# A group norm kernel on one core: one weight load for all the identity matmuls instead of one before each

## The chip, the cores and the metric

The kernel runs on one core of one Trainium2 chip, with the other cores idle. The metric is the device time of one execution in microseconds.

## The reference, cut to what matters

```python
x: (128, 1024, 32, 16) bf16;  g, b: (1024,) bf16;  G = 32 groups
xr  = x.reshape(B, G, C // G, H, W)
mu  = xr.mean(axis=(2, 3, 4));  var = ((xr - mu) ** 2).mean(axis=(2, 3, 4))
out = (xr - mu) / sqrt(var + 1e-5) * g + b          # bf16
```

The input is 134 MB and the output as much again. Each byte must be read once and written once.

## The kernel before

The work is cut into 32 tiles of 128 partitions by 16384 elements (4 MiB). Each partition is one (image, group) pair. Six slots of a ring hold the tiles; each is loaded, normalised in place and stored. For the mean, each partition's row has to be summed. TensorE does part of that: it multiplies by the identity matrix and accumulates twelve chunks of 512 columns in PSUM (the memory that TensorE writes its sums to), so that 6144 columns become 512. VectorE folds the other 10240 columns into one number beside them ("pair sum"), and ScalarE adds up the 513 results. Then ScalarE makes the sum of squares in two halves and VectorE scales the tile in place.

```python
NT = 32; SLOTS = 6; PE_CHUNKS = 12; MM_FREE = 512; PS_BUFS = 3

# SyncE: load(j) -> ring slot j % 6; store(i) waits for done, then writes; six stores are queued at the end

def on_tensor(e):
    e.wait_ge(s_eye, 2)
    e.wait_ge(s_gb, 32)
    e.matmul(out=gb_p[:], lhsT=rep[:], rhs=gb_b[:], start=True, stop=True).then_inc(s_gbp, 1)

    def one(c, t):                                   # tile of slot c in round t
        for k in range(PE_CHUNKS):
            if k == 0:
                e.wait_ge(ld[c], (t + 1) * 16)       # the tile has landed
            elif k == PE_CHUNKS - 2:
                e.wait_ge(meaned[(c - 2) % SLOTS], t + 1)
            elif k == PE_CHUNKS - 1:
                e.wait_ge(paired, t * SLOTS + (c + 1))   # VectorE's pair sum is there
            mm = e.matmul(
                out=sums(c), lhsT=eye[:],
                rhs=slot(c)[:, k * MM_FREE : (k + 1) * MM_FREE],
                start=(k == 0), stop=(k == PE_CHUNKS - 1),
            )                                        # emits a weight load and a matmul
            if k == 0:
                mm.then_inc(first_in, 1)             # lets VectorE start the pair sum
        mm.then_inc(summed[c], 1)                    # lets ScalarE take the mean
    in_rounds(e, one)

# ScalarE per tile: wait summed; mean; square of half 0; square of half 1; variance; square root
# VectorE per tile i: pair(i + 1); wait for the root of tile i; scale and bias; 32 x tensor_scalar in place
# ... (cut)
```

## Time and profile before

| | before |
|---|---|
| device time, median of the first 3 runs | 632.58 us (632.29 to 632.61) |
| profiled span | 631.1 us |
| DMA, share of the span | 99.0%, 268.44 MB |
| VectorE / ScalarE / TensorE busy | 84% / 80% / 25% |
| weight loads | 385, 49.9 us busy |

The page of the kernel before starts with busy times (PE is the matmuls, PEld the weight loads that run beside them, DVE is VectorE, ACT ScalarE, POOL GpSimd), then the span in 40 slices, then the DMA queues, then the groups of instructions. A group line has busy time and mean duration in ns, and behind the second bar the idle time before it and what ended it ("issue" where the profile shows nothing that was waited for). `ring` holds the tiles, `eye` is the identity, `ps` the sums, `jp` belongs to the pair sum and `jm` to the mean:

```profile
span 631.1 us, 2973 instructions
PE 158.2 (25%) x380; PEld 49.9 (8%) x385; DVE 529.4 (84%) x1185; ACT 504.0 (80%) x258; POOL 1.0 (0%) x8
...
DMA  8999999999999999999999999999999999999996
GB/s 366 432 432 413 434 434 430 438 432 432 432 432 432 430 432 432 434 430 434 432 432 428 432 432 430 432 432 432 426 432 432 432 434 432 434 434 434 438 410 263
...
q1 hardware_dynamic: 9648, 268.44, 99.0%
...
L184 PE MATMUL ps<-ring,eye 128*128 128x512 bf16 x379 | 158.0, 589 | 423.9 <-DVE jp L243 292.0
...
L184 PEld LDWEIGHTS ps<-ring,eye 128*128 128x128 bf16 x384 | 49.8, 137 | 531.8 <-DVE jp L243 313.5
```

Read it so: DMA is full in every slice but the first and the last, at 410 to 438 GB/s in all of these. TensorE idles 424 us before its matmuls, and the larger part of that ends when VectorE's pair sum arrives. (Five matmul records are missing from this trace: 379 of 384.)

A burst in the timeline of the kernel before: the twelfth matmul of one tile, which waited for the pair sum, and behind it the first eleven of the next (start, duration, engine, line, what, count; in brackets the idle time in front). The granted clock in this stretch was 0.50:

```profile
53.45 0.13 PEld L184 LDWEIGHTS ps<-ring,eye 128*128 128x128 bf16 x2 [17.26 <-DVE jp L243]
53.46 5.30 PE L184 MATMUL ps<-ring,eye 128*128 128x512 bf16 x12 [16.77 <-DVE jp L243]
...
53.86 0.15 PEld L184 LDWEIGHTS ps<-ring,eye 128*128 128x128 bf16 x1 [0.28 <-issue]
...
54.29 0.15 PEld L184 LDWEIGHTS ps<-ring,eye 128*128 128x128 bf16 x1 [0.27 <-issue]
```

The loads follow each other every 0.43 us, are 0.15 us long, and leave 0.28 us in between. Twelve matmuls in 5.30 us are eleven steps of 0.427 us and one whole duration of 0.61 us. The question is whether the 0.427 us contain any of the load.

The chain of waits of the kernel before, in the tail (start, duration, what):

```profile
522.30 29.25 DMA ring<-in_x_dram
551.55 0.04 issue
551.60 0.62 PE ps L184
...
592.66 0.62 PE ps L184
593.30 0.70 ACT jm L205 x2
```

Here the last tiles are computed with no more loads to come. The chain meets TensorE at a tile's first matmul and at twelfth matmuls that follow a wait, each 0.62 us long.

### The profile page before, as it was taken

How to read it: one execution, taken by the hardware profiler on the slowest of the kernel's cores; microseconds unless marked ns; L12 is line 12 of the kernel's file. 1: busy time of each engine (PE TensorE's matmuls, PEld its weight loads, DVE VectorE, ACT ScalarE, POOL GpSimd, SP SyncE). 2: the span in 40 equal slices, each digit the busy share in tenths (PEclk: the TensorE clock that was granted, in tenths of full speed). 3: DMA queues.
4: the chain of work that ended last, by engine and by line, in shares of the span. 5: the costliest groups of instructions: out<-in, count | busy, mean ns of one | idle time of the engine just before them, and what ended most of it. 6: DMA issues, size and time to landing. Idle time of an engine off the chain costs nothing.

```text
span 631.1 us, 2973 instructions
## 1 busy us (share of the span) xinstructions
PE 158.2 (25%) x380; PEld 49.9 (8%) x385; DVE 529.4 (84%) x1185; ACT 504.0 (80%) x258; POOL 1.0 (0%) x8
## 2 busy tenths in 40 slices
PE   1523333222233330331063014203220430052000
PEld 0101111000010110110011001101000110010000
DVE  1579999999999999699689959995998699599963
ACT  0798999999999999699948977894999499859960
POOL 0000000000000000000000000000000000000000
PEclk9766555666665665666565557656665665576555
DMA  8999999999999999999999999999999999999996
GB/s 366 432 432 413 434 434 430 438 432 432 432 432 432 430 432 432 434 430 434 432 432 428 432 432 430 432 432 432 426 432 432 432 434 432 434 434 434 438 410 263
DMA packets 9744, 268.44 MB, mean 425 GB/s; under 512 B 1168, under 2 KB 1168, under 8 KB 1168
## 3 DMA queue, kind: packets, MB, share of 16 engines
q1 hardware_dynamic: 9648, 268.44, 99.0%
q10 hardware_dynamic: 96, 0.00, 0.0%
HBM read 134.22 MB, written 134.22 MB: 425 GB/s over the span
## 4 chain that ended last, share of the span: by engine, by line
ACT 50%; DMA 34%; DVE 6%; issue 5%; PE 2%; DVEq 2%; SPq 0%
ACT ja L213 46%; DMA out_dram<-ring 18%; DMA ring<-in_x_dram 16%; DVE ring L276 5%; PE ps L184 2%; ACT jm L205 2%; DVEq L259 1%; ACT var L223 1%; ACT std L227 1%; DVE jp L243 1%; DVEq L262 0%; DVEq L264 0%; DVE bia L270 0%; DVE scl L266 0%; DVEq L243 0%
## 5 line engine op out<-in xcount | busy, mean ns | idle before, releaser
L213 ACT ACTIVATE ja<-ring,nm 128x8192 fp8e5<-128x8192 bf16 x64 | 455.8, 7122 | 2.1
L276 DVE TENSOR_SCALAR ring<-ring,scl,bia x1024 | 333.5, 405 | 1.2
L184 PE MATMUL ps<-ring,eye 128*128 128x512 bf16 x379 | 158.0, 589 | 423.9 <-DVE jp L243 292.0
L243 DVE SCALAR_TENSOR_TENSOR jp<-ring 128x5120 fp8e5 (+1 forms) x32 | 175.7, 5492 | 61.4 <-PE ps L184 49.4
L205 ACT ACTIVATE jm<-ps 128x513 fp8e5<-128x513 f32 x32 | 19.3, 602 | 99.0 <-PE ps L184 99.0
L184 PEld LDWEIGHTS ps<-ring,eye 128*128 128x128 bf16 x384 | 49.8, 137 | 531.8 <-DVE jp L243 313.5
L264 DVE RECIPROCAL rstd<-std 128x1 f32 x32 | 6.3, 196 | 11.9 <-ACT std L227 11.9
L213 ACT ACTIVATION_READ_ACCUMULATOR ja<-ring,nm 128x1 f32 x64 | 11.9, 186 | 0.0
L270 DVE SCALAR_TENSOR_TENSOR bia<-scl,nm,gb 128x32 f32<-128x32 f32 x32 | 8.0, 250 | 4.2
L227 ACT ACTIVATE std<-sq,var 128x1 f32<-128x1 f32 x32 | 9.4, 295 | 1.0
L223 ACT ACTIVATE var<-sq,eps_t 128x1 f32<-128x1 f32 x32 | 9.4, 294 | 1.0
L255 DVE COPY gb<-gb_p 128x64 f32<-128x64 f32 x1 | 0.2, 225 | 11.3 <-PE gb_p L173 11.3
L266 DVE TENSOR_SCALAR scl<-gb,rstd 128x32 f32<-128x32 f32 x32 | 7.7, 241 | 1.1
L205 ACT ACTIVATION_READ_ACCUMULATOR jm<-ps 128x1 f32 x32 | 6.2, 194 | 0.0
L243 DVE DVE_READ_ACCUMULATOR jp<-ring (+1 forms) x32 | 4.5, 140 | 0.0
L173 PE MATMUL gb_p<-gb_b,rep 32*128 32x64 bf16 x1 | 0.2, 207 | 11.1 <-DMA gb_b<-in_b_dram 11.1
L201 ACT ACT_TABLE_LOAD x1 | 1.3, 1283 | 1.9 <-issue 1.9
L173 PEld LDWEIGHTS gb_p<-gb_b,rep 32*128 32x128 bf16 x1 | 0.1, 100 | 11.1 <-issue 11.1
L155 POOL TENSOR_SCALAR_AFFINE_SELECT rep<-ones_b 32x128 bf16<-32x128 bf16 x1 | 0.3, 304 | 0.0
L151 POOL TENSOR_SCALAR_AFFINE_SELECT eye<-ones_b 128x128 bf16<-128x128 bf16 x1 | 0.3, 294 | 0.4 <-issue 0.4
L201 ACT ACTIVATE warm<-eps_t 128x1 f32<-128x1 f32 x1 | 0.2, 203 | 0.0
L145 POOL MEMSET ones_b<- 128x128 bf16 x1 | 0.2, 205 | 0.5 <-SPq L283 0.5
(5 smaller groups left out, 0.5 us busy)
## 6 DMA issues: line engine op xcount, KB each, us to landing
ring<-in_x_dram SPq DMA_DIRECT2D x32, 4096.0 KB, 29.2
out_dram<-ring SPq DMA_DIRECT2D x31, 4096.0 KB, 31.5
out_dram<-ring SPq DMA_DIRECT2D x4, 1024.0 KB, 6.9
gb_b<-in_g_dram ACTq DMA_DIRECT2D x1, 2.0 KB, 6.3
gb_b<-in_b_dram ACTq DMA_DIRECT2D x1, 2.0 KB, 9.5
```

Of the source, the lines that this page charges most:

```text
L184: mm = e.matmul(out=sums(c), lhsT=eye[:], rhs=slot(c)[:, k * MM_FREE : (k + 1) * MM_FREE], start=(k == 0), stop=(k == PE_CHUNKS - 1),)
L201: e.activation(out=warm[:], in_=eps_t[:], func=ACT.Sqrt)
L205: e.activation(out=jm[:], in_=sums_and_pairs(c), func=ACT.Identity, scale=-inv_n, accum_out=nm[:, c : c + 1], saturate=False,).then_inc(me ...
L213: e.activation(out=ja[:], in_=slot(c)[:, h * (F // 2) : (h + 1) * (F // 2)], func=ACT.Square, bias=nm[:, c : c + 1], scale=1.0, accum_out= ...
L223: e.activation(out=var[:], in_=sq[:, 0:1], func=ACT.Identity, bias=eps_t[:], scale=inv_n).then_inc(varred[c], 1)
L227: e.activation(out=std[:, c : c + 1], in_=sq[:, 1:2], func=ACT.Sqrt, bias=var[:], scale=inv_n).then_inc(stded, 1)
L243: e.scalar_tensor_tensor(out=jp[:], in0=part(i, lo, n), scalar=1.0, in1=part(i, lo + n, n), op0=ALU.mult, op1=ALU.add, accum_out=ps[:, bas ...
L259: e.drain()
L264: e.reciprocal(out=rstd[:], in_=std[:, bass.ds(i % SLOTS, 1)]).then_inc(inverted, 1)
L266: e.tensor_scalar(out=scl[:], in0=gb[:, 0:KC], scalar1=rstd[:], scalar2=None, op0=ALU.mult).then_inc(scaled, 1)
L270: e.scalar_tensor_tensor(out=bia[:], in0=scl[:], scalar=nm[:, bass.ds(i % SLOTS, 1)], in1=gb[:, KC : 2 * KC], op0=ALU.mult, op1=ALU.add,). ...
L276: ts = e.tensor_scalar(out=a, in0=a, scalar1=scl[:, k : k + 1], scalar2=bia[:, k : k + 1], op0=ALU.mult, op1=ALU.add,)
```

## The change

The identity is always the same weight matrix, so it need not be loaded again for each matmul. The intent is to take 383 of 385 weight loads out of TensorE's stream. The matmuls are emitted as bare instructions that use whatever weights are in the array (with two loads for 385 matmuls the result is correct).

```diff
+        e.ldweights(eye[:])
+
+        def add_up(to, chunk, k):
+            return e.add_instruction(
+                mybir.InstMatmult(
+                    name=nc.get_next_instruction_name(), engine=e.engine,
+                    start_tensor_calc=(k == 0),
+                    stop_tensor_calc=(k == PE_CHUNKS - 1),
+                    ins=[e.lower_ap(chunk), e.lower_ap(eye[:])],
+                    outs=[e.lower_ap(to)],
+                    tile_size=(P, P), tile_position=(0, 0),
+                    ldweights=False,
+                )
+            )
 ...
-                mm = e.matmul(
-                    out=sums(c), lhsT=eye[:],
-                    rhs=slot(c)[:, k * MM_FREE : (k + 1) * MM_FREE],
-                    start=(k == 0), stop=(k == PE_CHUNKS - 1),
-                )
+                mm = add_up(sums(c), slot(c)[:, k * MM_FREE : (k + 1) * MM_FREE], k)
```

One side effect is not in the diff: a wait ahead of a matmul used to sit on that matmul's weight load, the first of the two instructions. Now it sits on the matmul. The traces show it: in the bursts above and below, the 17.26 us of idle time that end with VectorE's pair sum stand in front of a load before the change, and 10.23 us in front of a matmul after it.

## The prediction

> **What bounds the kernel now.** The DMA queues. The page's slices show the DMA engines at 9 tenths nearly throughout, at 430 to 438 GB/s in most; the queue table gives 99.0% of 16 engines' span to the one queue that moves all 268.44 MB. At 432 GB/s that alone takes 268.44 MB / 432 GB/s = 621 us (an estimate) of the 631.1 us span. The other 10 us are the first slice (366 GB/s) and the last two (410 and 263 GB/s), where the last tiles are still computed. [...] TensorE is busy 25%; it waits 292 us for VectorE's pair sum and 131 us for loads. ScalarE (80%) and VectorE (84%) do not bind in the middle either.
>
> **What the change removes.** 383 of the 385 weight loads, 49.9 us busy at 137 ns each, for one load ahead of the first tile (about 0.1 us, in idle time before 13.4 us). Nothing moves: the emitted order on every engine is otherwise the same, and so are the waits, except that they sit on the matmul instead of the weight load before it.
>
> **How much is exposed.** Weight loads run beside matmuls. In the timeline at clock 0.50 they follow each other every 0.43 us (0.15 busy, 0.28 idle), and a burst of 12 matmuls takes 5.30 us: 11 x 0.427 + 0.61. [...] inside a burst a weight load already costs nothing. Only one that follows a wait can be exposed: a tile's first (waits for data) and twelfth (waits for the pair sum). I estimate at most 0.1 us each, the duration of a lone weight load.
>
> **On the critical path.** In the middle, DMA sets the pace and TensorE's 0.2 us a tile vanish in slack. Only the tail can show it. The chain there: tile 29's load lands at 551.6, first matmul (0.62), pair sum on VectorE (5.5), VectorE's loop of 17.2 us a tile (10.4 scaling, 5.5 pair, small ones), the last tile's twelfth matmul at 592.66 (0.61), ScalarE's squares, scaling, the last store. TensorE is on it twice: 0.2 us at most.
>
> **Prediction.** 632.4 us (before 632.58), range 631.6 to 633.2. Chances: faster by over 2% 0.01, within 2% 0.98, slower by over 2% 0.01.
>
> **What would show it right.** Weight loads 385 -> 2, PEld busy 49.9 -> about 0.2 us. Matmul spacing at clock 0.50 still 0.43 us, PE busy 150 to 158 us. DMA still 99%, 432 GB/s in the middle. ScalarE's squares still 7.12 us, VectorE's scaling 405 ns. First matmul to pair sum start in tile 0: 0.65 us now, perhaps 0.55. The tail from tile 29's landing to the end, 79.5 us, shorter by 0.2 us or less. TensorE's waits grow by what its work shrinks.
>
> **What would make it wrong.** If a matmul without its own weight load were slower or could not overlap its predecessor, bursts would grow past 5.3 us, but even 4 us more a tile stays within TensorE's slack of 14 us. If fewer TensorE instructions changed the granted clock, only the bursts would change. A different DMA rate, not caused by the change, is the likeliest source of a difference above 0.5 us.

## The result, and the profile after

| | before | after |
|---|---|---|
| device time, median of 4 runs | 632.43 us (632.19 to 632.61) | 632.27 us (632.05 to 632.44) |
| profiled span | 631.1 us | 630.7 us |
| weight loads, busy | 385, 49.9 us | 2, 0.2 us |
| DMA share of the span | 99.0% | 99.1% |

The ratio of after to before is 0.9997, with a 95% interval of 0.998 to 1.0015: the same time. Ratios here are the mean time of one kernel's fast runs over that of the other's of the same rounds, so they are not quite the ratio of the medians quoted. The result is correct.

The page after, the lines that answer to those above:

```profile
span 630.7 us, 2595 instructions
PE 156.7 (25%) x385; PEld 0.2 (0%) x2; DVE 529.6 (84%) x1185; ACT 504.0 (80%) x258; POOL 1.0 (0%) x8
...
DMA  8999999999999999999999999999999999999996
GB/s 366 432 432 409 434 436 432 432 434 434 428 432 432 432 434 430 434 430 432 432 432 428 432 432 432 432 432 432 432 432 432 432 426 432 430 430 436 432 421 271
...
q1 hardware_dynamic: 9648, 268.44, 99.1%
...
L178 PE MATMUL ps<-ring,eye 128*128 128x512 bf16 x384 | 156.5, 581 | 424.9 <-DVE jp L254 292.5
```

A burst in the timeline of the kernel after, at the same granted clock of 0.50:

```profile
575.09 5.28 PE L178 MATMUL ps<-ring,eye 128*128 128x512 bf16 x12 [10.23 <-DVE jp L254]
```

The chain of waits of the kernel after, in the tail:

```profile
522.25 29.00 DMA ring<-in_x_dram
551.25 0.04 issue
551.29 0.60 PE ps L178
...
592.33 0.60 PE ps L178
592.96 0.70 ACT jm L216 x2
```

The 49.7 us of weight loads are gone, and little else has moved. A burst of twelve is 5.28 us instead of 5.30: eleven steps of 0.427 us as before, and a lone duration of 0.59 us instead of 0.61. In the tail each meeting with TensorE is 0.60 us instead of 0.62. From tile 29's first matmul to the end of the span are 631.07 - 551.60 = 79.47 us before and 630.72 - 551.29 = 79.43 us after, one profile each. ScalarE's squares (7122 ns each) and VectorE's scaling (333.5 and 333.7 us in all) are as they were.

### The profile page after: what moved, and what is told of

Same layout as the page of the kernel before. It is cut to its first block, busy times and chain, and to the rows that moved or that the text cites. A ratio compares the mean times of both kernels' runs of the same rounds, so it can differ in the third digit from the quotient of the medians.

```text
span 630.7 us, 2595 instructions
## 1 busy us (share of the span) xinstructions
PE 156.7 (25%) x385; PEld 0.2 (0%) x2; DVE 529.6 (84%) x1185; ACT 504.0 (80%) x258; POOL 1.0 (0%) x8
## 3 DMA queue, kind: packets, MB, share of 16 engines
q1 hardware_dynamic: 9648, 268.44, 99.1%
## 4 chain that ended last, share of the span: by engine, by line
DMA 44%; ACT 40%; DVE 7%; issue 4%; PE 2%; DVEq 2%; SPq 0%
ACT ja L224 37%; DMA out_dram<-ring 28%; DMA ring<-in_x_dram 16%; DVE ring L287 6%; PE ps L178 2%; ACT jm L216 2%; DVEq L270 1%; ACT var L234 1%; ACT std L238 1%; DVE jp L254 1%; DVEq L273 0%; DVE bia L281 0%; DVE scl L277 0%; DVEq L275 0%; DVEq L254 0%
## 5 line engine op out<-in xcount | busy, mean ns | idle before, releaser
L224 ACT ACTIVATE ja<-ring,nm 128x8192 fp8e5<-128x8192 bf16 x64 | 455.8, 7122 | 2.1
L287 DVE TENSOR_SCALAR ring<-ring,scl,bia x1024 | 333.7, 413 | 1.2
L178 PE MATMUL ps<-ring,eye 128*128 128x512 bf16 x384 | 156.5, 581 | 424.9 <-DVE jp L254 292.5
## 6 DMA issues: line engine op xcount, KB each, us to landing
ring<-in_x_dram SPq DMA_DIRECT2D x32, 4096.0 KB, 29.1
out_dram<-ring SPq DMA_DIRECT2D x4, 1024.0 KB, 7.0
```

Of the source, the lines that this page charges most:

```text
L178: return e.add_instruction(mybir.InstMatmult(name=nc.get_next_instruction_name(), engine=e.engine, start_tensor_calc=(k == 0), stop_tensor ...
L224: e.activation(out=ja[:], in_=slot(c)[:, h * (F // 2) : (h + 1) * (F // 2)], func=ACT.Square, bias=nm[:, c : c + 1], scale=1.0, accum_out= ...
L287: ts = e.tensor_scalar(out=a, in0=a, scalar1=scl[:, k : k + 1], scalar2=bia[:, k : k + 1], op0=ALU.mult, op1=ALU.add,)
```

## The experiments

There are two layers that could hide a weight load, and the result alone doesn't tell them apart:

- **Theory A**: a load costs TensorE nothing, since it runs under the matmul in front of it. Only a load that has no matmul to hide under is seen.
- **Theory B**: a load does cost TensorE time, but TensorE has so much slack here that nobody sees it.

For the exposed place there is also **theory C**, the one that the prediction used: an unhidden load costs its whole duration of 0.1 us.

### 1. TensorE made the bound, matmuls of 512 columns

Each tile gets 108 extra matmuls into a spare PSUM tensor, in both kernels: with their own loads in before (bound512_load), without in after (bound512_none). The results stay correct.

```diff
+    spare = nc.alloc_psum_tensor("spare", [P, MM_FREE], F32)
 ...
                 if k == 0:
                     mm.then_inc(first_in, 1)
+                    for n in range(EXTRA):           # 108
+                        xx = e.matmul(               # bound512_none: add_up(...), no load
+                            out=spare[:, 0:COLS], lhsT=eye[:],      # COLS = 512
+                            rhs=slot(c)[:, 0:COLS], start=True, stop=True,
+                        )
```

> Before, plus 108 extra 128x512 matmuls a tile into a spare bank, each with its own weight load, so that TensorE becomes the bound. Theory A (a weight load runs under the matmul in front of it, so it is free even where TensorE is the bound): 120 matmuls of 0.216 us at full clock = 25.9 us a tile, about 830 us for 32 tiles plus 50 us of start and tail, 880 us, the same as bound512_none within 1%. Theory B (a weight load costs TensorE time, and the change gave nothing only because TensorE has slack): about 0.1 us more for each of 3840 loads, so some 380 us above bound512_none.

> After, with the same 108 extra matmuls a tile, without weight loads. A: about 880 us, the ratio to bound512_load 0.99 to 1.00. B: about 880 us against 1260 us of bound512_load.

Measured: 878.63 us with 3841 loads (878.10 to 879.20) and 878.67 us with two (878.37 to 879.08), against 632.73 us of before in the same rounds. The busy line of the page of bound512_load:

```profile
PE 827.7 (94%) x3767; PEld 376.4 (43%) x3841; DVE 532.7 (61%) x1185; ACT 504.1 (57%) x258; POOL 1.0 (0%) x8
```

The same line of bound512_none:

```profile
PE 827.5 (94%) x3767; PEld 0.2 (0%) x2; DVE 532.8 (61%) x1185; ACT 504.2 (57%) x258; POOL 1.0 (0%) x8
```

TensorE is now the bound, at 94%, and 376 us of load time have come out without any trace in the total. 827.7 us over 3840 matmuls are 0.2155 us each. Theory B asked for some 380 us; it falls. The runs show that the loads are free here (878.63 against 878.67 us), not by what means. Every load here brings the same matrix; no run puts a different one between two matmuls, so that case was not tested.

### 2. Shorter cover: 128 columns

Is it the length of the matmul that covers the load? The same edit, with EXTRA = 400 and COLS = 128.

> Before, plus 400 extra matmuls of only 128 columns a tile, each with its own weight load. Theory A says what hides a load is the length of the matmul in front: a matmul of 128 columns is about as short as a load or shorter, so part of each load must come out: spacing above 56 ns, somewhere from 80 to 105 ns, total about 1150 to 1450 us against 850 of bound128_none. B: spacing is the sum, about 0.16 us, total near 2150 us. If the load is free here too, both are at 850 us.

> After, with 400 extra matmuls of 128 columns a tile without weight loads: 400 x 0.056 + 12 x 0.216 = 25 us a tile, 800 us plus 50, about 850 us under both theories.

Measured: 854.00 us with loads (853.32 to 854.85), 848.44 us without (847.62 to 849.33). I expected at least 300 us between them and found 5.6 us, 0.4 ns for each of 12800 loads. The waits of TensorE's matmuls (total us, times, longest us), with loads (bound128_load):

```profile
PE ps L187 <- issue: 5.1, 5, 1.3
```

and without (bound128_none):

```profile
PE ps L181 <- issue: 0.2, 1, 0.2
```

So 4.9 of the 5.6 us are gaps in which TensorE waited for nothing that the profile shows. The stream itself ran at the same pace: 400 matmuls of 128 columns took 22.50 us with loads and as long without, 56 ns each. So the part of theory A that says "a short matmul cannot cover a load" fails at 128 columns, where a load is recorded at 98 ns and a matmul comes every 56 ns.

### 3. Shorter still: 64 columns

EXTRA = 700, COLS = 64, one timed round each.

> As bound128_load, with 700 extra matmuls of 64 columns a tile, each with its own load. Where does a load stop being hidden? In the run with four loads a matmul, loads followed each other about every 50 ns (at half clock)[...]. Theory A (the cover is the length of the matmul): here loads come out, the spacing is 40 to 55 ns, the total 32 x (700 x 0.040 to 0.055 + 2.6) + 50 = 1030 to 1370 us. If loads are free at any length, 740 us as bound64_none.

> Without the loads: 32 x (700 x 0.027 + 2.6) + 50 = 740 us under every theory, if the instructions arrive fast enough.

Measured: 1031.7 us with loads (1025.67 and 1037.71), 792.8 us without (792.48 and 793.03). The median with loads is just inside the range that I gave (its faster run is below it), and the reason that I gave is wrong. Without loads I expected 740 us: I had put in 27 ns, an estimate (an eighth of the 215.5 ns that a matmul of 512 columns took in experiment 1 is 26.9), for a matmul that takes 29.2 ns, which makes about 50 us over 22400. The timeline of the kernel with loads, the extra matmuls of one tile:

```profile
105.59 7.66 PE L197 MATMUL spare<-ring,eye 128*128 128x64 bf16 x257
117.08 5.44 PE L197 MATMUL spare<-ring,eye 128*128 128x64 bf16 x128 [3.83 <-issue]
123.55 3.89 PE L197 MATMUL spare<-ring,eye 128*128 128x64 bf16 x128 [1.03 <-issue]
129.48 3.89 PE L197 MATMUL spare<-ring,eye 128*128 128x64 bf16 x128 [2.03 <-issue]
```

and the kernel without:

```profile
107.55 20.58 PE L181 MATMUL spare<-ring,eye 128*128 128x64 bf16 x700
```

Without loads, 700 matmuls run through at (20.58 - 0.2) / 699 = 29.2 ns. With loads, a stretch of 257 runs at (7.66 - 0.2) / 256 = 29.1 ns, and those of 128 in 3.89 us at 29.1 ns: the same pace, so the load is still free inside a stretch (0.2 us is the mean duration of one, 198 ns on the page). What is lost are the gaps of 1 to 4 us between the stretches. The waits of the kernel with loads add them up:

```profile
PE spare L197 <- issue: 168.4, 76, 4.4
...
PE ps L187 <- issue: 5.8, 5, 1.3
```

The kernel without loads has 4.4 us of such gaps. The profiled spans are 1024.0 and 791.0 us, 233 us apart. So about 170 of these are TensorE standing with no visible reason. The rest, 63 us, is more busy time (804.0 against 740.8 us); in part it goes with a lower clock. The stretch with 5.44 us for 128, after the gap of 3.83 us, ran at a mean granted clock of 0.68, the one with 3.89 us that starts at 123.55, after a gap of 1.03 us, at 1.00, and the mean over the run was 0.926 against 0.979.

Two things point to the supply of instructions. 128 pairs are 256 instructions, and 70 of the 81 gaps come after a multiple of 128 pairs, give or take one. And the DMA queue marked "instruction" moved 188 packets in this run, against 98 without loads, 113 and 58 in the pair with 128 columns, and 5 and 3 in that with 512.

A third stands in the DMA records of the kept trace: each of the 81 gaps ends 1.1 to 1.7 us after a packet of that queue has landed, wherever in or before the gap the packet falls. Of instants picked at random, one in nine does so. The gap of 3.83 us, for instance, ends at 117.08; the packet before it started at 114.7 and took about 1 us. The few gaps of the kernel without loads and of the pair with 128 columns (5, 5 and 1) come at most once in each round of the loop, which is six tiles, and end 1.5 to 2.2 us after such a packet. So it is very likely that TensorE waits for its instructions here. It remains an inference: no run took the supply away by itself, and nothing shows why the packets come late.

### 4. The exposed place, magnified

In the tail a lone matmul is 0.02 us shorter without a load in front. Here each tile gets 60 extra matmuls of 512 columns, each of which waits for the one in front to have finished. In the third variant a load is issued ahead of the wait, so that the load doesn't wait.

```diff
                     for n in range(EXTRA):           # 60
+                        e.ldweights(eye[:])          # serial2_early only
+                        if n:
+                            e.wait_ge(burned, t * (SLOTS * EXTRA) + (c * EXTRA + n))
                         xx = e.matmul(...)           # serial2_load: wait sits on its load
+                                                     # _none, _early: add_up(...), no load
+                        xx.then_inc(burned, 1)
```

> Before, plus 60 extra 128x512 matmuls a tile, each of which waits for the one in front to have finished, so nothing runs for its weight load to hide under, and the wait sits on the load. Magnifies the exposed place 1920 times. In the traces of before and after the lone twelfth matmul took 0.62 and 0.60 us, 20 to 25 ns apart. Theory A (only the wait for an unhidden load comes out): 1920 x 20 to 25 ns = 38 to 48 us above serial2_none. Theory C (the prediction's 0.1 us each, the whole duration of a load): 190 us above. Absolute time between 950 and 1460 us, depending on the clock that such a chain is granted.

> After, with the same 60 serialised extra matmuls a tile, without loads. The floor of this set: 38 to 48 us under serial2_load in theory A, 190 us in theory C.

> serial2_none, with a weight load ahead of each extra matmul's wait: as many loads as serial2_load, but the wait sits on the matmul, so the load may run while the matmul in front is at work. If what is exposed comes of where the wait sits, equal to serial2_none within 1%. If each load costs time anywhere in such a chain, equal to serial2_load.

| | weight loads | median | range |
|---|---|---|---|
| serial2_load | 2305 | 1002.21 us | 1001.08 to 1002.65 |
| serial2_none | 2 | 966.66 us | 965.67 to 967.16 |
| serial2_early | 1922 | 965.84 us | 965.68 to 967.04 |

By the means of the runs, the loads on which a wait sits cost 1002.04 - 966.54 = 35.5 us. The first of a tile's 60 has no wait, which leaves 32 x 59 = 1888 links and 18.8 ns for each, at a granted clock of 0.985 to 0.986. That is a little under the 20 to 25 ns that I read off the tail, and far from theory C's 0.1 us. The same loads issued ahead of the wait cost nothing (965.84 against 966.66 us without them). The group of load instructions of serial2_load (the number behind "x" is the count, then busy us and mean ns):

```profile
L201 PEld LDWEIGHTS spare<-ring,eye 128*128 128x128 bf16 x1920 | 183.0, 95 | 692.8 <-PE spare L201 689.1
```

and that of serial2_early:

```profile
L210 PEld LDWEIGHTS <-eye 128*128 128x128 bf16 x1920 | 184.1, 96 | 732.9 <-issue 729.3
```

Both spend the same 183 to 184 us on loads. In the first the load is released by the matmul in front of it, in the second it waits for no one. The cost of a load in a chain is thus set by where the wait sits, and even then a fifth of its recorded 95 ns comes out.

### 5. Four loads for each matmul

```diff
+                for _ in range(3):
+                    e.ldweights(eye[:])
                 mm = e.matmul(
```

> Before, with three more weight loads ahead of each of the 384 matmuls: four loads each, more than one matmul may be able to hide. Total 632.4 us, the same as before within 0.3%: TensorE has about 14 us of slack a tile, so even a burst that grows from 5.3 us to 8 or 9 us stays hidden. If loads were what paced the kernel anywhere in the middle, the total would rise by up to 32 x 3 us = 100 us.

Measured: 633.17 us (633.05 to 633.31) against 633.00 us of before in the same rounds, ratio 1.0002 (0.9986 to 1.0019). The total holds, but my picture of the burst was too dark: I expected it to grow to 8 or 9 us. The timeline of one:

```profile
53.93 4.76 PE L186 MATMUL ps<-ring,eye 128*128 128x512 bf16 x12 [16.14 <-DVE jp L245]
...
54.52 0.10 PEld L186 LDWEIGHTS ps<-ring,eye 128*128 128x128 bf16 x1
54.76 0.24 PEld L185 LDWEIGHTS <-eye 128*128 128x128 bf16 x3
54.95 0.10 PEld L186 LDWEIGHTS ps<-ring,eye 128*128 128x128 bf16 x1
```

Groups of four loads come 0.43 us apart, the pace of the matmuls at half clock. Four loads fit under one matmul here. (The burst is shorter than 5.30 us; its mean granted clock was 0.57, where the burst of the kernel before had 0.50.) So this run shows that the loads don't matter to the total, but not by the slack that I had named for it.

### 6. The DMA bound taken away

Finally, is it really DMA that sets the pace? All tiles but the last store only their first half.

```diff
-                    out=o_v[i][:, p * w : (p + 1) * w], in_=slot(i)[:, p * w : (p + 1) * w]
+                    out=o_v[i][:, p * w : p * w + v], in_=slot(i)[:, p * w : p * w + v]
+                    # v = w for the last tile, w // 2 for all others
```

> Before, storing only the first half of each tile but the last (wrong result on purpose): 3 of 4 bytes moved. If DMA sets the pace, the time falls to that of the next in line, VectorE's 17.2 us a tile: 36 us of start + 32 x 17.2 + 11 us for the last store = about 600 us. If it stays at 632 us, DMA was not the bound.

> After, with the same cut. TensorE's lone twelfth matmul is now inside a loop that VectorE paces with no slack of its own, but ScalarE has about 1.4 us of slack a tile there: equal to halfstore_load within 0.2%. If TensorE's 20 ns a tile came through, 0.6 us faster; if 0.1 us a tile did, 3 us faster.

Measured: 588.19 us (588.05 to 588.26) before and 588.12 us (587.97 to 588.15) after, where the whole kernel took 632.73 us. The line of the DMA queue on the page of halfstore_load:

```profile
q1 hardware_dynamic: 9648, 203.43, 83.4%
```

Taking 65 MB of 268 MB away saved 44 us and left DMA 83.4% busy instead of 99.0%, so DMA was the bound; then VectorE is (90% busy, one tile every 17.24 us). ScalarE is 86% busy, but it idles 1.40 us a tile for the twelfth matmul, which waits for VectorE's pair sum. TensorE's twelfth matmul is in the loop of each tile now, 20 ns shorter in each of 32, and still doesn't show: 0.07 us between the medians. The timeline of halfstore_load says where it goes:

```profile
328.14 0.29 ACT L228 ACTIVATE std<-sq,var 128x1 f32<-128x1 f32 x1
328.99 0.14 DVE L244 DVE_READ_ACCUMULATOR jp<-ring  x1
328.99 0.20 DVE L265 RECIPROCAL rstd<-std 128x1 f32 x1
329.18 0.13 PEld L185 LDWEIGHTS ps<-ring,eye 128*128 128x128 bf16 x2 [13.52 <-DVE jp L244]
```

ScalarE's root is ready at 328.14 + 0.29 = 328.43, and VectorE takes it up 0.56 us later, as it is still at its pair sum. The same place in halfstore_none:

```profile
328.07 0.29 ACT L239 ACTIVATE std<-sq,var 128x1 f32<-128x1 f32 x1
328.95 0.14 DVE L255 DVE_READ_ACCUMULATOR jp<-ring  x1
328.95 0.20 DVE L276 RECIPROCAL rstd<-std 128x1 f32 x1
```

Here the root waits from 328.36 to 328.95, 0.59 us. What TensorE hands on sooner only lengthens that wait.

## Why the prediction was right, and where it was off

- **DMA bounds the kernel**: right. 99.0% and 99.1% of the span, 432 GB/s in most slices of both profiles. With a quarter of the bytes gone, the time fell by 44 us.
- **Weight loads inside a burst are free**: right, though the trace of before alone did not show it, since every burst in it has its loads; in the prediction it was my estimate. The result and experiment 1 show it: a burst's steps are 0.427 us with loads and without, and with TensorE as the bound, 3841 loads and 2 gave 878.63 and 878.67 us.
- **The exposed term, "at most 0.1 us each, the duration of a lone weight load"**: as an upper bound it held, and such a load is exposed; but not for its whole duration. A lone matmul went from 0.61 to 0.59 us in the traces, and the magnified chain gave 18.8 ns. Two such places in the tail are 0.04 us, not 0.2 us. The pair sum of tile 0 starts 0.62 us after the first matmul (13.60 to 14.22), where the prediction hoped for 0.55 from 0.65.
- **The total, 632.4 us**: measured 632.27, inside the range. Between before and after lie 0.16 us, less than the spread of either kernel's four runs (0.4 us), so no run resolves a gain. That 0.16 us is close to the forecast gain of 0.18 us is luck: what the traces of the tail account for is 0.04 us.
- **"If a matmul without its own weight load were slower"**: it isn't. A burst at clock 0.50 took 5.28 us, and the mean granted clock was 0.598 in the profiled runs of both kernels.
- **"TensorE's waits grow by what its work shrinks"**: roughly. The idle time before its matmuls went from 423.9 to 424.9 us, its busy time from 158.2 to 156.7 us (with five matmul records missing before).
- **The slack of 14 us a tile** was never called upon: even four loads a matmul didn't lengthen a burst's pace, so this argument, though it may hold, was not tested.

Still open is what holds up the instructions in experiment 3. Each gap there ends just after an instruction packet has landed, but the supply was not isolated by a run.

## What to carry to other kernels

Before removing an instruction, look at the spacing of its neighbours and not at its busy time: 49.9 us of weight loads stood in spacings that already were those of matmuls alone. In these runs removing them was worth something where a wait sits on the load in a chain that sets the time (18.8 ns a load in experiment 4; issuing the load ahead of the wait gave the same), or, it seems, where short matmuls use up instructions faster than they come (1031.7 against 792.8 us with 64 columns). And when a number comes out as expected, look at the timeline all the same: the 64 column run hit its range for a reason that was not the one given.
